# Six identity products behind the pack-query attention product of the first three head groups

## Chip, cores and metric

The kernel runs on one core of one Trainium2 chip. The metric is device time in microseconds (us); lower is better.

## What is computed

Attention through 32 packed queries per head, and two expert layers behind it:

```python
def sm_attn(qq, kk, vv):
    s = scale * np.matmul(qq, kk.transpose(0, 1, 3, 2))
    s = s - np.max(s, axis=-1, keepdims=True)
    a = np.exp(s)
    a = a / (np.sum(a, axis=-1, keepdims=True) + 1e-09)
    return np.matmul(a, vv)
p_packed = sm_attn(p, k, v)              # (4, 8, 32, 64)
out = sm_attn(q, p_packed, p_packed)     # (4, 8, 576, 64)
...
x = attn_out.transpose(0, 2, 1, 3).reshape(B * S, H * D)   # 2304 x 512
h = x @ w_in                             # d_ff 2048
g = np.maximum(h, 0.0) + np.log1p(np.exp(-np.abs(h)))
x = g @ w_out
gate = 1.0 / (1.0 + np.exp(-(x @ w_gate)))   # d_ff 1536
val = x @ w_val
return gate * val @ w_out2
```

## The kernel before

The four batches and eight heads are worked in eight units: unit u is batch u // 2 and four of its heads. `attn_unit(u)` is a generator of eleven stages, parted by `yield`. In order it transposes k (L347, copied out at L354), forms the scores of p (L378), takes their softmax (L386 to L398, the exponential on ScalarE at L389), transposes q (L347), transposes the softmax (L412, copied out at L413), multiplies it with v (L431), copies that product's blocks into `bdT` on ScalarE (L94, called from `copy`), forms the scores of q against `bdT` (L455), takes their softmax (L465 to L473, its last product on GpSimd), and, two empty stages later, transposes the result (L483) into `A2h` and `A2l` (L489 and L99).

The product with v goes to a PSUM tile `pp` of 128 x 512 float32, one bank, out of a pool of four (`bank1`). It fills columns 0 to 127; the copies into `bdT` read those. Columns 128 to 511 are not used.

`att_tick` runs one stage of one live unit. At the start, units 0 and 1 are run out by themselves, with unit 2 begun. From then on the stages of later units are put between the products of the first expert layer: `emit_h` (three products of split float32r parts, L111 to L113, on `Wp`, which `prep_wp_one` makes at L560 out of `bdT` and `w_in`), then abs, exp, ln on ScalarE (L613 to L615), the activation's end on VectorE (L623), and `emit_out1` (L641, L642, L644), summed on VectorE (L96 or L649). The weights come as float64 and are converted on VectorE (L178, L183, L187). The second expert layer follows, in Winograd's form (L111 to L113 again, by tile `bank`) with its output product at L965 to L967.

Each engine works through one queue in order. The queues' order is set when the program is built, out of the written order and the dependencies, and is not always the written one. An engine waits at a tile for the last instruction that it depends on.

Of the kernel before, what the change touches and what calls it, by code (L numbers as in the profile page):

```python
# [16 lines left out]
DRAM = bass.MemoryType.DRAM  # L17
# [3 lines left out]
def attn_moe_moe_kernel(  # L21
# [10 lines left out]
    w_out2: bass.AP,  # L32
    out: bass.AP,
):
    # float32 operands of the large products are split exactly into two
    # float32r parts (12 significant bits each): x = hi + lo, and a product is
    # hi*hi + hi*lo + lo*hi, accumulated in float32.
    #
    # The attention's second product is folded into w_in per batch:
    # (A2 @ pp) @ w_in = A2 @ (pp @ w_in), pp having 32 rows a head.  # L40
    #
    # Tokens of a batch are kept in the order (c, r) for token 6 r + c.
    nc = tc.nc
    B, H, S, D = q.shape
    NK = p.shape[2]
# [3 lines left out]
    P = 128  # L49
# [30 lines left out]
    cv = ctx.enter_context(tc.tile_pool(name="cv", bufs=NCV))  # L80
    wo_p = ctx.enter_context(tc.tile_pool(name="wo", bufs=4))

    # The layers' sums; queries, keys and values before those.
    xa = cst.tile([P, KD * NT], F32, name="xa")

    def bank2():
# [30 lines left out]
    att = tc.alloc_tile_pool(name="att", bufs=1, side="right")  # L117
    ph1 = tc.alloc_tile_pool(name="ph1", bufs=1, side="left")

# [1 line left out]
    # A weight's float64 words come as pairs of int32, in tiles of 512 columns.  # L121
    w32 = {
        nm: w.bitcast(I32)
        for nm, w in (
            ("in", w_in), ("out", w_out), ("g", w_gate), ("v", w_val), ("o2", w_out2)
        )
    }
    # Some of the second layer's are converted during the first and kept in DRAM.
    later = {f: [(nm, f // 2, f % 2) for nm in ("g", "v", "o2")] for f in range(2 * NCH2)}
    early = list(EARLY)  # L130
    order, early_in = [], {}
# [10 lines left out]
    def load_next():  # L142
        if not waiting:
            return
        nm, c, f = key = waiting.popleft()
        if XR and key == ("out", 0, 0):
            # The sums' tile is free until the first of them.
            t = xa[:, : 2 * DM].bitcast(I32).rearrange("p (n t) -> p n t", t=2)
        else:
            t = raw.tile([P, KD * P, 2], I32, tag="raw", name="raw_" + nm)  # L150
        a = c * CF + f * P
        if nm in ("out", "o2"):
            nc.sync.dma_start(t.rearrange("p n t -> p (n t)"), w32[nm][a : a + P, :])
        else:
            nc.sync.dma_start(
                t.rearrange("p (k n) t -> p k (n t)", k=KD),
                w32[nm][:, 2 * a : 2 * (a + P)].rearrange("(k p) x -> p k x", p=P),
            )
        raws[key] = t
# [1 line left out]
    cps = [CPS > 1]  # L161

    def convert(key, dst):
        # float64 -> float32 of the same value's leading 24 bits: sign and
        # exponent's first bit, seven bits of exponent with 20 of the mantissa,
        # three more of the mantissa.
        t = raws.pop(key)
        hw, lw = t[:, :, 1], t[:, :, 0]
        if len(dst.shape) == 3:
            hw = hw.rearrange("p (k n) -> p k n", k=KD)  # L170
            lw = lw.rearrange("p (k n) -> p k n", k=KD)
        to = x = dst.bitcast(I32)
        if cps[0] and dst.space != PSUM:
            x = bank1()
            if len(dst.shape) == 3:
                x = x.rearrange("p (k n) -> p k n", k=KD)
            x = x.bitcast(I32)
        nc.vector.tensor_scalar(  # L178
            x, hw, 3, 0x3FFFFFF8, op0=ALU.logical_shift_left, op1=ALU.bitwise_and
        )  # L180
        if not cps[0]:
            yield
        nc.vector.scalar_tensor_tensor(  # L183
            x, hw, -0x40000000, x, op0=ALU.bitwise_and, op1=ALU.bitwise_or
        )
        yield
        nc.vector.scalar_tensor_tensor(  # L187
            to, lw, 29, x, op0=ALU.logical_shift_right, op1=ALU.bitwise_or
        )
        load_next()  # L190
# [7 lines left out]
        split_lo(nc.gpsimd, lo, x, hi)  # L198
        return hi, lo

    # Queries, keys and values take the accumulators' slots before those are
    # needed; a slot's next tile is loaded behind its last use.
    PLACE = {
        0: "345", 1: "621", 2: "345", 3: "634", 4: "563", 5: "456",
        6: "565", 7: "656",
# [33 lines left out]
    def done_kqv(nm, u):  # L239
        for tag, key in list(busy.items()):  # L240
            if key == (nm, u):
                del busy[tag]
        load_kqv()

    # Work that goes in between the large products' instructions.
    jobs = deque()

    idle = deque()
# [9 lines left out]
        while any(nm == name for nm, _ in jobs):  # L258
            tick()

# [1 line left out]
    ident = cst.tile([P, P], F32, name="ident")  # L262
    make_identity(nc, ident)
    # lhsT of pp @ w_in: for a head pair, [2 heads x d, 2 batches x 2 heads x keys],
    # zero off a head's own block.
    bdT = ph1.tile([P, 2 * B + 2, P], F32, name="bdT")
    # lhsT of the scores of p: zero off a head's own block.
    pT = [att.tile([P, 4 * P], F32, name=f"pT{i}") for i in range(2)]
    for t in pT:
        nc.gpsimd.memset(t, 0.0)  # L270
    nc.gpsimd.memset(bdT, 0.0)

# [1 line left out]
    A2h = [big.tile([P, 2, S], F32R, tag="big", name=f"A2h{b}") for b in range(B)]  # L274
    A2l = [big.tile([P, 2, S], F32R, tag="big", name=f"A2l{b}") for b in range(B)]
    praw = {}
# [46 lines left out]
    RELD = 0  # L323
    SUMP = 0
    E1 = nc.scalar

    def heads(tile_, start, step):
        # Two blocks of 32 columns, a step apart.
        return tile_[:, start : start + 2 * step].rearrange("p (j x) -> p j x", x=step)[
            :, :, :NK  # L330
        ]

    def by_chunk(src, j):
        # Two heads of a chunk of tokens side by side.
        x = att.tile([CT, NC, 2, D], F32, tag="x", bufs=2, name="x")
        nc.gpsimd.tensor_scalar(
            x, src[:, 2 * j : 2 * j + 2].rearrange("p h c d -> p c h d"), 1.0, 0.0,
            op0=ALU.mult, op1=ALU.add,
        )
        return x  # L340

    def tr_pair(src, j, dst, eng):
        x = by_chunk(src, j)
        for hf in range(2):
            ps = bank1()
            for c in range(3):
                nc.tensor.transpose(  # L347
                    ps[:, c * CT : (c + 1) * CT],
                    x[:, 3 * hf + c].rearrange("p h d -> p (h d)"),
                    ident[:CT, :CT],  # L350
                )
            o = dst[:, j, hf * HS : (hf + 1) * HS]
            if eng is nc.scalar:
                eng.activation(o, ps[:, :HS], AF.Copy)  # L354
            else:
                eng.tensor_copy(o, ps[:, :HS])

    def attn_unit(u):
        b, g = divmod(u, 2)
# [60 lines left out]
        for j in range(2):  # L420
            for c in range(NC):
# [7 lines left out]
                for e in range(2):  # L429
# [6 lines left out]
                        stop=c == NC - 1,  # L436
                    )
        done_kqv("v", u)
        for e in range(2):
            r = slice(64 * e, 64 * e + 64)  # L440
            to = bdT[r].rearrange("p j n -> p (j n)")
            copy(
                BDA, heads(to, 512 * half + 256 * g + 64 * odd + 32 * e, 64 if odd else 192),
                heads(pp[r], 32 * e, 64),
            )
# [49 lines left out]
    live = []  # L495

    def att_left(u):
        # Stages until the units up to u are done.
        return sum(STAGES - n for _, n, x in live if x <= u) + STAGES * sum(
            x <= u for x in units  # L500
        )
# [7 lines left out]
        return n not in NEEDS or (NEEDS[n], u) in kqv  # L509

    def att_tick(last=2 * B):
        # Two units at a time, some stages apart.
        if units and ready(units[0], 0) and units[0] <= last and (
            not live or (len(live) < (NLV if last < 8 else 2) and min(x[1] for x in live) >= (G0 if len(live) == 1 and last < 8 else GP if last < 8 else GAP))
        ):
# [8 lines left out]
                    live.append(x)  # L524
                return

# [1 line left out]
    w_in_f, wo_hl, Wp = {}, {}, {}  # L528

    def x2(b, s):  # L530
        # The first layer's sums, transposed, for half a batch of tokens.
        i = KD * HS * (2 * b + s)
        return xa[:, i : i + KD * HS].rearrange("p (m t) -> p m t", m=KD)

# [122 lines left out]
                att_tick()  # L657
        tick()

    # The gates' and the values' products are one product [G V] = x2 [Wg Wv], by  # L660
    # halves of x2's columns and of a batch's tokens in Winograd's form with
    # seven products of halves:
    #   S1 = A21 + A22, S2 = S1 - A11, S3 = A11 - A21, S4 = A12 - S2
    #   T1 = B12 - B11, T2 = B22 - T1, T3 = B22 - B12, T4 = B21 - T2
    #   U = A11 B11 + S2 T2
    #   G1 = A11 B11 + A12 B21, V1 = U + S1 T1 + S4 B22
    #   G2 = U + S3 T3 + A22 T4, V2 = U + S3 T3 + S1 T1
    w2 = []
    NF = NCH2 * 2
    HB = B // 2  # L670
# [49 lines left out]
        split("S3", t)  # L720
        yield

    # A tile of the gates' and values' columns gives seven blocks of B: B11 and
    # B21, B22, T1 and T4, T3 and T2.
    def new_cv():
        return cv.tile([P, DM], F32, tag="cv", name="cv")

# [43 lines left out]
            yield  # L771

    def prep_B(ps, f):
        # The second pass reads the blocks back.
        if f in scratch:
            parts = [new_cv(), new_cv()[:, :CF], new_cv(), new_cv(), new_cv()]
            for x, a, n in places(parts):
# [16 lines left out]
            oh, ol,  # L794
        )

# [1 line left out]
    load_p(0, nc.scalar)  # L798
    load_kqv()
    for _ in range(4):  # L800
# [2 lines left out]
    n = 0  # L803
# [8 lines left out]
    jobs.append(("win1", prep_win(1)))  # L812
    jobs.append(("wp01", prep_wp_one(0, 1)))
    jobs.append(("wo1", prep_wo(1)))
    # Pairs of batches by columns; the first pair ends ahead of the other, which
    # leaves time for the second layer's preparation.
    entries = [(b, c) for b in range(B) for c in range(2)]
    groups = [(x, c) for c in range(2, NCH1 - 2) for x in range(2)]
    groups += [(x, c) for x in range(2) for c in range(NCH1 - 2, NCH1)]
# [52 lines left out]
                    between(m, ticks)  # L872
            pend.append((b, c, s))

# [1 line left out]
    if PRE:  # L876
        tc.keep_in_program_order(nc.scalar.preload_act_table_set("sigmoid_and_others"))
    while pend:
# [168 lines left out]
```

## Time and profile before

| | us |
|---|---|
| median of 3 runs | 874.49 |
| lowest, highest | 873.87, 879.49 |
| span of the profiled execution | 870.41 |
| TensorE busy in it | 841.8 (97%) |
| mean granted TensorE clock | 0.992 |

Of the profiled execution only its span, from the first to the last instruction, is known as its own time; the timed runs count what lies around the span as well, and are other executions. PE is TensorE's matmuls, PEld its weight loads, DVE VectorE, ACT ScalarE, POOL GpSimd, SP SyncE. Matmuls are pipelined, so a merged row's time counts the overlap of a product with the one ahead of it once, and the step from one start to the next is shorter than one product's time.

### The profile page before, as it was taken

What the parts mean: (1) busy time and instruction counts of PE and PEld (TensorE: products, weight loads), DVE (VectorE), ACT (ScalarE), POOL (GpSimd) and SP (SyncE); (2) the same over time, 40 slices, a digit from 0 to 9 for tenths busy, and PEclk for the clock granted to TensorE, in tenths of its full rate; (3) what the DMA queues carried; (4) which work ended last, traced back from release to release, by engine and by line L of the source; (5) the groups of instructions that cost most, each with busy time, mean ns of one, the idle gap of its engine ahead of it and who ended that gap; (6) DMA issues with size and microseconds to landing.
All of it is one profiled execution on the core that took longest, in us unless ns stands there. A gap on an engine that the chain in (4) does not pass through costs nothing.

```text
span 870.4 us, 15541 instructions
## 1 busy us (share of the span) xinstructions
PE 841.8 (97%) x6064; PEld 790.2 (91%) x6064; DVE 618.2 (71%) x1047; ACT 401.8 (46%) x721; POOL 473.4 (54%) x455
## 2 busy tenths in 40 slices
PE   6889999999999999999999999999989999999997
PEld 5778989989999999999989999999979999999995
DVE  2886556747476857758798688898898746667665
ACT  4557565656666656677633431232342432322210
POOL 4544333254646455476469787886983534436400
PEclk9979999999999999999999999999999999999999
DMA  9774320112032402310056555644424213213004
GB/s 242 197 207 113 83 66 19 49 49 73 25 98 91 134 1 98 110 43 1 2 154 193 162 168 153 188 128 150 153 75 143 82 47 92 67 43 109 14 1 109
DMA packets 58010, 85.55 MB, mean 98 GB/s; under 512 B 6353, under 2 KB 39249, under 8 KB 57937
## 3 DMA queue, kind: packets, MB, share of 16 engines
q1 hardware_dynamic: 57648, 84.49, 33.8%
q8 instruction: 48, 0.79, 0.4%
q14 instruction: 26, 0.20, 0.1%
q10 hardware_dynamic: 288, 0.07, 0.0%
HBM read 65.67 MB, written 18.87 MB: 97 GB/s over the span
## 4 chain that ended last, share of the span: by engine, by line
PE 81%; DVE 9%; DMA 3%; ACT 3%; POOL 2%; issue 1%; SPq 0%; DVEq 0%; ACTq 0%; POOLq 0%
PE bank L113 9%; PE bank L112 9%; PE bank L111 9%; PE ps L641 6%; PE ps L642 6%; PE ps L644 6%; PE ps L967 5%; PE ps L965 5%; PE ps L966 5%; PE ps L113 3%; PE ps L111 3%; PE ps L112 3%; PE ps L578 2%; PE ps L455 2%; DVE aop L99 2%
## 5 line engine op out<-in xcount | busy, mean ns | idle before, releaser
L111 PE MATMUL bank<-aop,BH 128*128 128x288 f32 x672 | 198.7, 296 | 2.8 <-DVE work L918 1.0
L112 PE MATMUL bank<-aop,BH 128*128 128x288 f32 x672 | 197.9, 295 | 1.0 <-DVE aop L99 0.9
L113 PE MATMUL bank<-aop,BL 128*128 128x288 f32 x672 | 198.7, 296 | 0.1
L99 POOL TENSOR_TENSOR ghl<-g,ghl 128x576 fp32r<-128x576 f32 x64 | 93.7, 1465 | 138.8 <-ACT ghl L106 134.4
L649 DVE TENSOR_TENSOR xa<-xa,ps 128x288 f32<-128x288 f32 x224 | 98.1, 449 | 76.9 <-PE ps L644 76.8
L641 PE MATMUL ps<-ghl,woh 128*128 128x288 f32 x512 | 149.2, 306 | 2.5 <-DVE xa L649 2.4
L642 PE MATMUL ps<-ghl,wol 128*128 128x288 f32 x512 | 143.9, 296 | 0.0
L111 PEld LDWEIGHTS bank<-aop,BH 128*128 128x128 f32 x672 | 126.2, 188 | 8.0 <-issue 1.2
L112 PEld LDWEIGHTS bank<-aop,BH 128*128 128x128 f32 x672 | 126.4, 188 | 5.1 <-DVE aop L99 1.6
L113 PEld LDWEIGHTS bank<-aop,BL 128*128 128x128 f32 x672 | 126.5, 188 | 0.4 <-POOL BL L99 0.4
L99 POOL TENSOR_TENSOR BL<-cv,BH 128x512 fp32r<-128x512 f32 (+1 forms) x96 | 117.6, 1241 | 7.2 <-ACT BH L106 6.1
L644 PE MATMUL ps<-ghl,woh 128*128 128x288 f32 x512 | 109.4, 295 | 0.0
L641 PEld LDWEIGHTS ps<-ghl,woh 128*128 128x128 f32 x512 | 96.9, 189 | 6.1 <-DVE xa L649 2.1
L642 PEld LDWEIGHTS ps<-ghl,wol 128*128 128x128 f32 x512 | 97.0, 190 | 0.5
L918 DVE TENSOR_TENSOR work<-work,bank 128x576 f32<-128x576 f32 (+1 forms) x100 | 71.0, 725 | 29.0 <-PE bank L113 28.4
L965 PE MATMUL ps<-oh,gv 128*128 128x512 f32 x216 | 84.6, 392 | 1.3 <-DVE xa L973 0.8
L966 PE MATMUL ps<-ol,gv 128*128 128x512 f32 x216 | 84.8, 393 | 0.0
L967 PE MATMUL ps<-oh,gv 128*128 128x512 f32 x216 | 84.7, 393 | 0.0
L644 PEld LDWEIGHTS ps<-ghl,woh 128*128 128x128 f32 x512 | 82.7, 189 | 0.0
L973 DVE TENSOR_TENSOR xa<-xa,ps 128x512 f32<-128x512 f32 x90 | 61.5, 683 | 27.4 <-PE ps L967 26.9
L947 ACT ACTIVATE work<-bank 128x576 f32<-128x576 f32 (+1 forms) x25 | 15.8, 633 | 137.2 <-DVE bank L918 137.2
L113 PE MATMUL ps<-A2h,wpl 128*128 128x288 f32 x256 | 76.3, 298 | 2.9 <-POOL wpl L99 2.0
(121 smaller groups left out, 1745.8 us busy)
## 6 DMA issues: line engine op xcount, KB each, us to landing
cv<-B SPq DMA_DIRECT2D x52, 256.0 KB, 2.7
B<-cv SPq DMA_DIRECT2D x48, 256.0 KB, 2.9
raw_in<-in_moe_w_in_dram SPq DMA_DIRECT2D x16, 512.0 KB, 4.0
raw_out<-in_moe_w_out_dram SPq DMA_DIRECT2D x16, 512.0 KB, 3.7
raw_g<-in_moe_w_gate_dram SPq DMA_DIRECT2D x12, 512.0 KB, 4.1
raw_v<-in_moe_w_val_dram SPq DMA_DIRECT2D x12, 512.0 KB, 4.4
raw_o<-in_moe_w_out_dram SPq DMA_DIRECT2D x12, 512.0 KB, 4.2
xa<-in_q_dram SPq DMA_DIRECT2D x6, 576.0 KB, 6.6
```

Of the source, the lines that this page charges most:

```text
L99: eng.tensor_tensor(lo, x, hi.bitcast(F32), op=ALU.subtract)
L111: nc.tensor.matmul(ps, wh, xh, start=first, stop=False)
L112: nc.tensor.matmul(ps, wh, xl, start=False, stop=False)
L113: nc.tensor.matmul(ps, wl, xh, start=False, stop=last)
L641: nc.tensor.matmul(out_, wh[:, ms], gh[:, f], start=f == 0, stop=False)
L642: nc.tensor.matmul(out_, wl[:, ms], gh[:, f], start=False, stop=False)
L644: nc.tensor.matmul(out_, wo_hl[c, f][0][:, ms], gl[:, f], start=False, stop=f == 1)
L649: nc.vector.tensor_tensor(dst, dst, out_, op=ALU.add)
L918: nc.vector.tensor_tensor(to, x, y, op=ALU.add)
L965: nc.tensor.matmul(bank, gh[:, ts_], oh, start=f == 0, stop=False)
L966: nc.tensor.matmul(bank, gh[:, ts_], ol, start=False, stop=False)
L967: nc.tensor.matmul(bank, gl[:, ts_], oh, start=False, stop=f == 1)
```

## The change

`WARM = 3` and a function `warm` are new. In units 0, 1 and 2, right behind the product with v and ahead of the copies into `bdT`, six products of the identity with itself (float32, 128 x 128 by 128 x 128) are written into the last 128 columns of `pp`. Nothing reads them. Comments of the file are blanked out, and nothing else changes.

```diff
     E1 = nc.scalar
+    WARM = 3
...
+    def warm(u, to, n):
+
+
+        if u < WARM:
+            for _ in range(n):
+                nc.tensor.matmul(to, ident, ident, start=True, stop=True)
 
     def attn_unit(u):
         b, g = divmod(u, 2)
...
                         stop=c == NC - 1,
                     )
         done_kqv("v", u)
+        warm(u, pp[:, 3 * P :], 6)
         for e in range(2):
             r = slice(64 * e, 64 * e + 64)
             to = bdT[r].rearrange("p j n -> p (j n)")
```

## Rows read from the trace of the kernel before

**Rows 1.** The page: span, and the granted TensorE clock in 40 slices.
```profile
span 870.4 us, 15541 instructions
...
PEclk9979999999999999999999999999999999999999
```

**Rows 2.** Windows of 25 us: busy time and count by engine, granted clock, DMA.
```profile
50.00:75.00 25.00, 23.46 (x203) 21.13 (x204) 18.67 (x41) 15.52 (x35) 11.84 (x11) 0.80 0.77 189
...
175.00:200.00 25.00, 23.01 (x153) 22.29 (x153) 12.29 (x24) 15.21 (x24) 11.95 (x11) 0.93 0.14 43
```

**Rows 3.** Windows of 0.5 us about the longer stretch at the lower clock.
```profile
50.00:50.50 0.50, 0.00 (x0) 0.00 (x0) 0.43 (x3) 0.50 (x2) 0.00 (x0) 0.70 0.05 18
...
60.00:60.50 0.50, 0.50 (x4) 0.50 (x3) 0.00 (x0) 0.43 (x1) 0.00 (x0) 0.56 1.03 223
```

**Rows 4.** Timeline of PE, 19 to 52 us: start, time, instructions, idle before.
```profile
19.87 1.24 PE L431 MATMUL ps<-a1T,xa 96*64 96x32 f32 x36 [0.39 <-ACT a1T L413]
21.85 0.86 PE L412 MATMUL ps<-ident,a 128*96 128x128 f32 x6 [0.73 <-DVE a L398]
...
24.65 1.59 PE L431 MATMUL ps<-a1T,xa 96*64 96x32 f32 x48
26.79 2.25 PE L455 MATMUL ps<-bdT,qT 128*96 128x64 f32 x24 [0.55 <-ACT bdT L94]
...
48.11 0.71 PE L347 MATMUL ps<-ident,x 96*128 96x96 f32 x6
51.52 4.10 PE L455 MATMUL ps<-bdT,qT 128*96 128x64 f32 x24 [2.69 <-ACT bdT L94]
```

**Rows 5.** The chain that ended last, 34 to 61 us: start, time, what.
```profile
34.26 0.84 POOL a L473
...
42.42 0.76 DVE g L623
...
55.62 0.96 PE ps L347 x6
...
56.60 1.51 PE ps L412 x6
58.11 1.91 PE ps L560 x8
60.02 0.54 PE ps L641
```

**Rows 6.** Timeline of ACT, 49 to 52 us.
```profile
49.10 0.74 ACT L389 ACTIVATE a<-ps,mx 128x576 f32<-128x576 f32 x1 [1.76 <-DVE mx L387]
...
50.41 0.20 ACT L94 ACTIVATE bdT<-ps 64x64 f32<-64x64 f32 x1
...
51.25 0.22 ACT L94 ACTIVATE bdT<-ps 64x64 f32<-64x64 f32 x1
```

**Rows 7.** The chain that ended last, later: the same products at the full clock.
```profile
96.07 2.01 PE ps L455 x24
98.08 0.50 PE ps L347 x6
99.89 0.66 PE ps L412 x6
...
155.67 1.04 PE ps L560 x8
...
170.31 0.86 PE ps L578 x4
```

**Rows 8.** The page, groups of instructions: a weight load of 128 x 128.
```profile
L111 PEld LDWEIGHTS bank<-aop,BH 128*128 128x128 f32 x672 | 126.2, 188 | 8.0 <-issue 1.2
```

**Rows 9.** Timeline of PE, two places: queue order at 61 us, a stall at 182 us.
```profile
61.45 0.29 PE L112 MATMUL ps<-A2l,wph 128*128 128x288 f32 x1
61.58 0.30 PE L641 MATMUL ps<-ghl,woh 128*128 128x288 f32 x1
...
182.27 0.40 PE L113 MATMUL ps<-A2h,wpl 128*128 128x288 f32 x1 [1.99 <-POOL wpl L99]
```

## Prediction

> **What bounds the kernel now.** I read the page first: the span, and the row of granted clocks [rows 1]. It is full nearly everywhere, but one slice early on shows 7 tenths. The windows of 25 us place what is lost: 0.80 of the clock between 50 and 75 us, and a smaller loss (0.93) between 175 and 200 us [rows 2]. From 75 us to the end TensorE is hardly ever idle, so time that it loses or gains early should arrive at the end: little behind it has slack. The finer windows put the drop inside the half microsecond from 50.0 (0.70 is full for 0.20 us and half for the rest, so at 50.20) and the return into the one from 60.0 (0.56, so near 60.44) [rows 3]. That is 10.2 us at 1.2 in place of 2.4 GHz.
>
> What stood ahead of the drop is in PE's own timeline [rows 4]: unit 2's transposes of q end at 48.82, and then TensorE is idle for 2.69 us, until the copies into bdT let the scores of q start at 51.52. The clock fell 1.4 us into that hole. The scores, transposes and weight products behind it ran at half speed, and the chain that ended last goes straight through them [rows 5]. ScalarE explains the hole [rows 6]: the product with v was done by 48.1, but the copies stand in ScalarE's queue behind an exponential that waits for VectorE until 49.10; they start at 50.41 and 51.25.
>
> The second loss is of the same kind: PE waits 1.99 us for GpSimd at 182.27 [rows 9], and the clock is low for some 3.4 us behind it (7% of a 25 us window at half is 14% of it [rows 2]). The change puts nothing there.
>
> **What one set of six costs.** The float32 products are two records each in this trace: unit 1's 24 products with v are x48, a unit's 12 products with bdT are x24 [rows 4]. So a set is 12 records of 128 moving columns with a 128 x 128 weight. The nearest rows at the full clock: four records of 256 columns in 0.86 us, so 0.108 us for 128 columns, and six transposes of 128 columns in 0.66 us, 0.11 us each [rows 7]. I take 12 x 0.11 = 1.3 us. The low end is the spacing of the smaller products against bdT, 2.01/24 = 0.084 us [rows 7], 1.0 us a set. The high end is a weight load that nothing hides, 0.188 us [rows 8], 2.3 us a set; I don't take it, since those loads lie under the products ahead of them.
>
> **Unit 0.** The product with v ends at 21.11 (19.87 + 1.24) and PE then waits 0.73 us for VectorE before unit 1's transposes [rows 4]. The set hides 0.7 of its 1.3 us in that wait; 0.6 us is left on the path. Ends: 0.3 and 1.6 us.
>
> **Unit 1.** The product with v ends at 26.24, and the scores of q start at 26.79 after the two copies [rows 4]. The only idle time is those copies' 0.55 us. If a copy may run while PE writes other columns of the same bank, the copies lie under the set, the scores start at 27.55, and the cost is 0.8 us. If the copies wait for the sixth product, the whole 1.3 us is added. I take 1.3 us: the copies are written behind the products and read the same tile, and the trace of before shows no engine reading a PSUM tile that PE is still filling. Ends: 0.5 (1.0 us a set, copies hidden) and 2.3 us.
>
> The Trainium skill bears on this in "PSUM — Partial Sum Buffer", section "PSUM bank collisions raise a hardware error": a write of TensorE and a read of ScalarE must not meet in one bank and quadrant. By that rule the copies have to be kept behind the set, 1.3 us rather than 0.8; no run here shows it yet.
>
> **Do those 1.9 us arrive?** Behind 26.79 the chain runs from the scores of q through the softmax (its last product on GpSimd at 34.26), into the first expert products, from their activation into VectorE's end of it at 42.42, and on through VectorE's and ScalarE's queues to the copies at 51.25 [rows 5, 6]. Each link there waits for the one ahead of it; none is a transfer that would come at a fixed time. I carry the 1.9 us through in full. Low end 0.9, if conversions of weights on VectorE slip into the wait.
>
> **Unit 2.** The product with v is done by 48.1, where q's transposes start [rows 4]; a set puts PE's end from 48.82 to about 50.1. The copies start at 50.41 because of what is ahead of them on ScalarE [rows 6], and q's transposes are copied out only behind the second copy at 51.25, so nothing waits: cost 0. The cover is ScalarE's queue; if it put the copies first, the set's 1.3 us would be on the path. What changes is the hole: 1.4 us (50.1 to 51.5) in place of 2.69, and it opens at about the point where the clock had fallen, not 1.4 us before it.
>
> **What the clock is worth.** On the chain the pieces at half clock are 4.10 (scores of q) [rows 4], 0.96, 1.51, 1.91 and 0.54 us [rows 5]: 9.0 us. At the full clock the same pieces are 2.01, 0.50, 0.66 and, for eight records of L560, 1.04 us [rows 7]; the last, a first product of a group, I halve to 0.3. That is 4.5 us, a difference of 4.5 us. With the scores done 2 us earlier, the transposes of q and of the softmax stand closer to ScalarE's copies of them; I take off 0.4 us for that wait. So 4.1 us if the clock stays up; the ends are 0 and 4.5.
>
> **Sum.** +0.6 +1.3 +0 -4.1 = -2.2 us. The profiled span is 870.41 us, and would be 868.2. The median of the runs, 874.49, lies 4.08 us above that span (the lowest run 3.46). I carry those 4.1 us over: 874.5 - 2.2 = 872.3 us.
>
> **Rivals.**
>
> (a) The clock falls all the same, and the kernel is slower. A hole of about 1.4 us is left in front of the scores of q, as the copies on ScalarE did not move. In the trace the clock dropped when PE had been idle for 1.4 us, which is just as long. For it: this near equality. Against it: holes of 0.73 and 0.55 us between the same kinds of products came without a fall [rows 4], and PE works without a break for longer ahead of the hole that is left. It decides from the point at which the hole left is again long enough for a fall. The price is the sets of units 0 and 1 with nothing in return, +1.9 us: 876.4.
>
> The Trainium skill, "TensorE: Matmul & The Clock Gate", section "What's actually happening", says that the point at which the clock changes is not tied to the kernel's start and differs between executions of one kernel. By that rule both (a) and my forecast would occur among the runs of one kernel, and the single profile of before cannot show how often; the spread of the runs of before, 873.87 to 879.49, is as wide as one such stretch (10.2 us at half, some 5 us) and agrees with it.
>
> (b) Another queue order. The order of PE's queue is not the written one: at 61.58 a product of the second weight stands among the three parts of the first [rows 9]. Eighteen more products can move what is built behind them. On the bad side the stall at 182 us, which costs 2.0 us of idle and, at half clock for 3.4 us, another 1.7, comes once more than now with the sets' cost: 874.5 + 1.9 + 3.7 = 880.1. On the good side that stall is gone on top of the forecast: 872.3 - 3.7 = 868.6.
>
> (c) The change does not do what it says: the products, which nothing depends on but the copies, are put elsewhere in PE's queue, say in front of a wait that hides them, or somewhere that leaves the hole. Then the time is that of before, 874.5. The write to pp ties them between the tile's first use and its release, so I give it little.
>
> **Chances.** My forecast 0.48; (a) 0.26; (b) bad 0.10, (b) good 0.11; (c) 0.05. The bounds of the unknown terms widen each of them: the forecast runs from 870.5 (0.3 and 0.5 on the path, 4.5 gained, gives 870.8) to about 874 (1.6 and 2.3 on the path and 4.1 gained gives 874.3), (a) from 875.4 to 878.4. A run of before can differ from another by 5 us. To leave out no more than 2 in 10 I go from 867.0, below (b) good, to 879.5, short of (b) bad. About what a measurement of this kernel can tell from no change is 1%, 8.7 us. Faster by over that means below 865.7: only (b) good with more than one stall gone, 0.04. Slower by over that means above 883.2: (b) bad with two more stalls, 0.05. Within: 0.91.
>
> **What would show it.** In the changed kernel's timeline of PE: twelve records behind each of the first three products with v, 1.3 us a set; unit 0's and unit 1's scores of q later by 0.6 and 1.9 us; the copies of unit 1 behind the set's last record; PE's idle time before unit 2's scores of q at 1.4 us; a granted clock of 1.00 from 50 to 65 us, and the scores of q there in 2.0 to 2.2 us rather than 4.1. The stall near 182 us and its low clock should stand as they do now. It would be wrong if the clock is low in that stretch again, if the sets cost 2 us each, or if waits appear behind 75 us that are not there now.

## The result

The changed kernel takes 868.33 us (median of 13 runs, 866.77 to 873.0); before it was 874.49 us in 13 runs beside them. The ratio is 0.9916, 95% interval 0.989 to 0.9941: faster by 0.6 to 1.1%. Run again beside other executions of before, it gave 867.84 us and 0.991 (0.9878 to 0.9943). The time lies in the forecast's range and the direction was right; the size was not, 6.2 us against 2.2. The change, 0.8%, is within the 1% that the forecast gave 0.91, though the interval reaches past it.

The page of the changed kernel, span and granted clock:

```profile
span 864.7 us, 15615 instructions
...
PEclk9999999999999999999999999999999999999999
```

Windows of 25 us (busy time by engine, granted clock, DMA), the two that lost clock in before [rows 2]:

```profile
50.00:75.00 25.00, 24.16 (x235) 21.79 (x234) 17.16 (x42) 16.34 (x39) 13.02 (x13) 1.00 0.82 193
175.00:200.00 25.00, 23.00 (x168) 22.38 (x167) 11.92 (x25) 15.29 (x25) 15.57 (x14) 1.00 0.13 41
```

Neither fall is there. The timeline of PE in the changed kernel answers to [rows 4]. Line numbers have moved: L364 is the new product, L439 the product with v, L464 the scores of q, L348 and L420 transposes.

```profile
20.12 1.24 PE L439 MATMUL ps<-a1T,xa 96*64 96x32 f32 x36 [0.40 <-ACT a1T L421]
21.29 1.60 PE L364 MATMUL ps<-ident 128*128 128x128 f32 x12
22.73 0.82 PE L420 MATMUL ps<-ident,a 128*96 128x128 f32 x6
...
27.20 1.60 PE L364 MATMUL ps<-ident 128*128 128x128 f32 x12
29.76 2.25 PE L464 MATMUL ps<-bdT,qT 128*96 128x64 f32 x24 [0.96 <-ACT bdT L94]
...
48.02 1.59 PE L439 MATMUL ps<-a1T,xa 96*64 96x32 f32 x48
49.54 1.60 PE L364 MATMUL ps<-ident 128*128 128x128 f32 x12
50.98 0.66 PE L348 MATMUL ps<-ident,x 96*128 96x96 f32 x6
52.31 2.25 PE L464 MATMUL ps<-bdT,qT 128*96 128x64 f32 x24 [0.67 <-ACT bdT L94]
54.40 0.66 PE L348 MATMUL ps<-ident,x 96*128 96x96 f32 x6
```

Each set is twelve records and 1.4 us from its start to the next instruction's. The hole ahead of unit 2's scores of q is 0.67 us, down from 2.69, and those scores take 2.25 us in place of 4.10. ScalarE's timeline in the changed kernel shows the copies into `bdT` behind the set:

```profile
22.99 0.45 ACT L94 ACTIVATE bdT<-ps 64x64 f32<-64x64 f32 x2 [2.33 <-PE ps L364]
...
28.84 0.22 ACT L94 ACTIVATE bdT<-ps 64x64 f32<-64x64 f32 x1 [2.38 <-PE ps L364]
...
51.83 0.43 ACT L94 ACTIVATE bdT<-ps 64x64 f32<-64x64 f32 x2
```

By the start times of the same instructions in the two profiles, the changed kernel is 0.25 us late before its first set (unit 0's product with v, 20.12 against 19.87), 0.88 late at unit 1's transposes of the softmax (22.73 against 21.85), 2.97 late at unit 1's scores of q (29.76 against 26.79), 0.79 late at unit 2's (52.31 against 51.52), and about 2.45 us early from 66 us on. That stays to 171 us. It becomes 4.0 us where before has its second low clock; PE's wait there is 2.00 us in the changed kernel too, and the clock does not fall behind it. Another 1.1 us comes near 211 us, where VectorE in before waits for a transfer of weights and in the changed kernel does not. The timelines of VectorE, first before, then the changed kernel:

```profile
211.49 0.69 DVE L178 TENSOR_SCALAR ps<-raw_out 128x512 int32<-128x512 int32 x1 [1.23 <-DMA raw_out<-in_moe_w_out_dram]
```
```profile
206.17 0.68 DVE L178 TENSOR_SCALAR ps<-raw_out 128x512 int32<-128x512 int32 x1
```

That transfer took 5.1 us from issue to landing in before and 3.6 us in the changed kernel. The like happens once more near 331 us and is worth 0.5 us. 2.45 + 1.55 + 1.1 + 0.5 makes 5.6 of the 5.7 us between the two spans.

### The profile page after: what moved, and what is told of

Its sections match the earlier page's. It is cut to its first block, busy times and chain, and to the rows that moved or that the text cites. A ratio compares the mean times of both kernels' runs of the same rounds, so it can differ in the third digit from the quotient of the medians.

```text
span 864.7 us, 15615 instructions
## 1 busy us (share of the span) xinstructions
PE 839.6 (97%) x6100; PEld 789.6 (91%) x6100; DVE 614.6 (71%) x1047; ACT 401.1 (46%) x721; POOL 473.2 (55%) x455
## 4 chain that ended last, share of the span: by engine, by line
PE 84%; DVE 7%; DMA 3%; ACT 2%; POOL 2%; issue 1%; SPq 0%; POOLq 0%; ACTq 0%; DVEq 0%
PE bank L113 9%; PE bank L111 9%; PE bank L112 9%; PE ps L650 7%; PE ps L651 7%; PE ps L653 7%; PE ps L976 5%; PE ps L975 5%; PE ps L974 5%; PE ps L113 4%; PE ps L111 4%; PE ps L112 4%; PE ps L587 2%; DVE aop L99 2%; PE ps L464 2%; PE ps L348 1%
```

## The experiments

All kernels are variants of the changed one, except the first. Each result gives every execution's mean granted clock beside its time, and that decides most of them. Places of a fall are known only for the profiled execution of each kernel. The table comes from the results; "low" is a mean clock below 0.987, "high" 0.996 and above (to three digits).

```
kernel                            median us  ratio to before (95%)     runs: low  between  high
before, beside all of these         875.02                               91:  26    61      4
changed                             868.33   0.9916 (0.9890-0.9941)      13:   0     2     11
changed, again                      867.84   0.9910 (0.9878-0.9943)       7:   0     0      7
before, again                       876.30   1.0010 (0.9982-1.0038)      12:   5     7      0
sets in units 0 and 1               870.05   0.9922 (0.9894-0.9950)       9:   0     7      2
sets in units 0 and 2               870.11   0.9953 (0.9927-0.9980)      12:   0     7      5
set in unit 0                       872.15   0.9970 (0.9949-0.9991)      12:   0    12      0
set in unit 1                       872.45   0.9980 (0.9947-1.0013)      12:   4     8      0
set in unit 2                       873.10   0.9979 (0.9948-1.0010)      12:   3     5      4
one column each                     878.16   1.0030 (1.0003-1.0058)      12:  11     1      0
sets in units 3, 4, 5               878.91   1.0038 (1.0010-1.0066)      12:   6     6      0
sets in banks of their own          871.91   0.9948 (0.9927-0.9969)      10:   0     3      7
one more set in the wait at 180     870.91   0.9941 (0.9916-0.9966)       8:   0     0      8
copies of unit 2 on VectorE         875.27   0.9988 (0.9961-1.0014)      12:   4     8      0
```

**Before, again.** No edit.

> The kernel of before once more, to see how its granted clock varies between executions. Theory A (the gain is TensorE's clock: a stretch at half speed near 50 us, and at times one near 183 us, that the products of unit 2 prevent): the mean granted clock is below 0.995 in nearly every run, 0.988 to 0.994, and the median is 874.5 us within 1. Theory B (the gain is the order of the queues, which is rebuilt when products are added; the clock is incidental): nothing else than the same time; the clock may be near 1.000 in many of the runs without their being faster.

876.3 us, clocks 0.982 to 0.992: 0.8 us above what theory A allowed, with lower clocks than it named in five of twelve. Over the 91 executions of before, the 26 low ones have a median of 880.0 us at 0.9815, the 61 between 874.2 at 0.991, the 4 high ones 870.3 at 0.996. The clock is not incidental: it orders the executions by time, over 10 us. This profile has a fall that mine of before had not. Windows and PE's timeline of before in this execution:

```profile
20.00:25.00 5.00, 3.58 (x59) 3.31 (x57) 4.03 (x9) 2.64 (x9) 0.10 (x1) 0.79 1.05 271
25.00:30.00 5.00, 4.45 (x74) 4.27 (x74) 2.91 (x7) 1.54 (x5) 1.52 (x2) 0.87 0.91 256
50.00:55.00 5.00, 2.31 (x51) 2.09 (x48) 4.66 (x11) 3.20 (x9) 0.48 (x1) 0.86 0.61 156
...
185.00:190.00 5.00, 4.52 (x23) 4.52 (x24) 0.91 (x2) 2.02 (x3) 4.16 (x4) 0.68 0.00 2
```
```profile
23.05 1.52 PE L412 MATMUL ps<-ident,a 128*96 128x128 f32 x6 [1.03 <-DVE a L398]
```

An early fall, 3.4 us from about 22.9 us, starts inside the wait behind unit 0's product with v: 1.03 us here, 0.73 in [rows 4].

This execution, at 0.989, is not one of the low ones. Its three falls make 17 us at half speed. A mean of 0.9815 takes some 32 us (an estimate: 2 x 0.0185 x 870). No low execution of before was profiled, so where the other 15 us lie no trace shows. That they belong to the early fall is inferred, from the variants in which unit 0's set takes the low executions away.

**Only unit 2.**
```diff
-        if u < WARM:
+        if u == 2:
```

> Only unit 2 has the six products. Theory A: the clock stays up from 50 to 60 us as in the changed kernel, and the sets of units 0 and 1 (0.8 us late at unit 2's scores of q in the changed kernel) are saved: 867.5 us, between 866 and 868.5. Theory B: the order of the first two units is that of before, so some of the gain goes: 869 to 874.

873.1 us: a miss for theory A by 5 us, and inside what theory B gave. The clock does stay up at unit 2's scores of q, with a hole of 1.40 us ahead of them. Four of twelve executions are at 0.996 or above, against 4 of 91 of before. But three of twelve are low, so what makes an execution low remains, and in the profile a wait at another place has a fall of 6.8 us behind it, from about 62.4 us:

```profile
61.72 0.40 PE L113 MATMUL ps<-A2h,wpl 128*128 128x288 f32 x1 [2.00 <-DVE wpl L99]
...
62.76 0.44 PE L113 MATMUL ps<-A2h,wpl 128*128 128x288 f32 x1
```

The second row is the same kind of product at half speed (0.44 against 0.29 us).

**Only units 0 and 1.**
```diff
-    WARM = 3
+    WARM = 2
```

> Units 0 and 1 have the six products, unit 2 has none. Theory A: the hole ahead of unit 2's scores of q is back and with it the half clock near 50 us; the two sets are paid for nothing: 875.5 us, between 874.5 and 877, mean clock below 0.995. Theory B: the queues are rebuilt from unit 0 on, as in the changed kernel, so most of the gain stays: 867 to 871.

870.05 us: theory A as I had put it falls. It had these two sets as a mere price, and they bring most of the gain. Theory B's number came true, but the clocks speak for a wider theory: no execution is low, and the fall near 50 us is shorter (6.8 us in the profile, from 52.0), behind a hole of 1.24 in place of 2.69 us:

```profile
51.56 3.73 PE L464 MATMUL ps<-bdT,qT 128*96 128x64 f32 x24 [1.24 <-ACT bdT L94]
```

**All three, one column each.**
```diff
-                nc.tensor.matmul(to, ident, ident, start=True, stop=True)
+                nc.tensor.matmul(to[:, :1], ident, ident[:, :1], start=True, stop=True)
```

> All eighteen products are there, but each moves one column instead of 128, so that the waits and very nearly the queue order of the changed kernel stay and the work is gone. Theory A: nothing fills the hole, the clock falls near 50 us: 874 us, between 872.5 and 875.5, clock below 0.995. Theory B: 867 to 869, and rather below the changed kernel, since the price of the products is gone.

878.16 us, slower than before and above what either theory gave. I had missed one thing, that these products take as long as the full ones:

```profile
21.11 1.50 PE L364 MATMUL ps<-ident 128*128 128x1 f32 x12
...
26.91 1.89 PE L364 MATMUL ps<-ident 128*128 128x1 f32 x12
29.34 4.11 PE L464 MATMUL ps<-bdT,qT 128*96 128x64 f32 x24 [0.54 <-ACT bdT L94]
```

So this kernel pays the price of all three sets, and the clock falls all the same, near 28, near 55 and, like the last one of before, near 188 us. Windows of the first two:

```profile
25.00:30.00 5.00, 4.46 (x70) 4.27 (x69) 2.47 (x7) 1.48 (x4) 0.41 (x1) 0.78 0.98 242
...
55.00:60.00 5.00, 4.04 (x26) 3.75 (x26) 3.46 (x8) 3.52 (x9) 0.92 (x1) 0.52 0.69 209
```

The expectation took it that this kernel has the changed kernel's queue order. It has not. Listed by start time in the traces, with the sets left out, the instructions of TensorE, VectorE, ScalarE and GpSimd come in exactly the order of before. The changed kernel's lists differ from that by 194 lines on TensorE, some 100 each on VectorE and ScalarE, and 34 on GpSimd. ScalarE's copies into `bdT` of unit 2 show it. They stand apart, with an activation between them, as in [rows 6], where the changed kernel has them together behind all three activations (51.83, above):

```profile
56.09 0.20 ACT L94 ACTIVATE bdT<-ps 64x64 f32<-64x64 f32 x1
...
56.93 0.22 ACT L94 ACTIVATE bdT<-ps 64x64 f32<-64x64 f32 x1
```

So this run says nothing against theory B. It is a clean comparison with before: the same order, eighteen narrow products more, a ratio of 1.003 (1.0003 to 1.0058), and the clock low in 11 of 12 executions against 26 of 91.

**Units 3, 4 and 5.**
```diff
-        if u < WARM:
+        if 3 <= u < 6:
```

> The three sets of six stand in units 3, 4 and 5, where TensorE has little idle time, and none in units 0 to 2. Theory A (the time follows the granted clock; the falls near 22 to 28, near 50 and near 183 us are what the sets prevent): all falls of before stay, and three sets of 1.5 us are on TensorE's path: 879 us, between 876.5 and 881, clock 0.98 to 0.993. Theory B (any rebuilt queue order of this kind is better than that of before): below 873.

878.91 us, as theory A has it: the falls of before stay. At like clocks the price can be read: its six executions at 0.990 to 0.992 have a median of 876.3 us against 874.6 for the 47 of before at these clocks, its six low ones 882.1 against 880.0. Three sets of 1.4 us cost 1.7 to 2.1 us there. Against theory B the run says little: its order hardly differs from that of before (26 lines on TensorE, 4 on GpSimd).

**Sets in banks of their own.**
```diff
-        warm(u, pp[:, 3 * P :], 6)
+        if u < WARM:
+            warm(u, bank1()[:, :P], 6)
```

> As the changed kernel, but each set writes a PSUM bank of its own, so that the copies into bdT no longer wait for it. Theory A: the same clock, and in units 0 and 1 the copies run under the set; the scores of q of unit 1 start some 1 us earlier: 867.3 us, between 866 and 868.5. A rival (the copies' wait costs nothing, later work hides it): 868.3, as the changed kernel. If the clock falls more often than there: 870 to 873.

871.91 us: neither the gain nor the tie came. The copies no longer wait, and unit 1's scores of q start 2.96 us behind the start of its product with v (24.89), in place of 4.09 us (25.67 to 29.76) in the changed kernel. But GpSimd's order is another, and a hole of 2.34 us opens a little later, with a fall of 6.8 us behind it:

```profile
27.85 2.17 PE L465 MATMUL ps<-bdT,qT 128*96 128x64 f32 x24
...
36.75 0.47 PE L493 MATMUL ps<-ident,a 96*128 96x96 f32 x3 [2.34 <-POOL a L483]
```

Being early was worth nothing: by 107 us this profile is 3.3 us behind the changed kernel's.

**One more set in the wait near 180 us**, nine products between the second and third part of the first product of that stage:
```diff
+                if (b, c, s, f, t) == (0, 2, 0, 0, 0):
...
+                    warm(0, ps[:, 1, 384:], 9)
```

> As the changed kernel, and nine more identity products, into unused columns, inside the 2.0 us for which TensorE waits near 180 us. Theory A: the fall of 3.4 us behind that wait, which most runs of the changed kernel seem to have (mean clock 0.998), is gone: mean clock 0.999 to 1.000 in most runs, 867.2 us, between 866 and 868. Rival (that fall costs next to nothing, or the products come too late to fill the wait): 868 to 869.

The clock came out as theory A said, 0.999 or 1.000 in seven of eight executions. PE's timeline shows 0.65 us of the wait left:

```profile
177.27 2.17 PE L364 MATMUL ps<-ident 128*128 128x128 f32 x18
180.09 0.40 PE L623 MATMUL ps<-A2h,wpl 128*128 128x288 f32 x1 [0.65 <-POOL wpl L99]
```

The time, 870.91, did not: in the profiles it is 0.3 us behind the changed kernel up to 170 us and 4.2 behind in the second expert layer, in three steps (near 180, 287 and 446 us). PE's waits for VectorE's sums rise from 1.5 to 2.7 us. What sets those steps off is open; a full clock does not by itself make the shorter time.

**Copies of unit 2 on VectorE, no products.**
```diff
-    WARM = 3
+    WARM = 0
...
-                BDA, heads(to, 512 * half + 256 * g + 64 * odd + 32 * e, 64 if odd else 192),
+                BDA and u != 2, heads(to, 512 * half + 256 * g + 64 * odd + 32 * e, 64 if odd else 192),
```

> No products at all; the copies of unit 2 into bdT are VectorE's, in whose queue they stand ahead of the softmax's later steps, so that the hole ahead of unit 2's scores of q gets shorter by itself. Theory A: the fall near 50 us goes or gets shorter and the early one near 22 us stays as in before: 871.5 us, between 869 and 874. Rival (the fall comes from the kinds of products there, not from the hole): 873.5 to 875.5, clock 0.991 as before.

875.27 us, no gain that can be told from none. The hole is 1.43 us and the clock falls in the profile from 50.6 for 6.8 us, in place of 10.2; four of twelve executions are low. The rival's time came (873.5 to 875.5), and theory A's shorter fall. The hole is about half as long, and the clock still falls, 0.5 us behind its end.

**The changed kernel again, and single sets.**

> The changed kernel once more, beside runs of before on the chip of these four, for its granted clocks. If the time follows the clock: mean clock 0.998 in most runs and 868.5 us, between 867 and 870, 6 to 7 us under before. If the first result was luck of a few runs: 870 or more.

867.84 us, all seven executions at 0.998 or 1.000.

```diff
-        if u < WARM:
+        if u == 0:
```

> Only unit 0 has its six products. Theory (before has an early fall near 22 us, in the wait of 0.7 to 1.0 us between unit 0's product with v and unit 1's transposes, and unit 0's set fills just that wait): the early fall is gone, the one near 50 us stays: 870.5 us, between 869 and 873, clock 0.993 or 0.994 in most runs and hardly any at 0.985 or below. Rival (the early fall starts behind unit 1): as before, 874 to 876, with clocks of 0.985 and below in a third of the runs.

872.15 us, as expected, and no execution low: unit 0's set alone takes those away. The late fall stays in full, behind 3.16 us:

```profile
52.26 4.11 PE L464 MATMUL ps<-bdT,qT 128*96 128x64 f32 x24 [3.16 <-ACT bdT L94]
```

```diff
-        if u < WARM:
+        if u == 1:
```

> Only unit 1 has its six products. Theory of unit 0's wait: the early fall stays, 874.5 to 877, with clocks of 0.985 and below in some runs. Rival (the early fall starts behind unit 1): 870 to 871.5, clock 0.993 or 0.994.

872.45 us, better than its theory, but four of twelve executions are low and the early fall stands in the profile (3.4 us from 21.7). What unit 1's set does is seen later: the hole ahead of unit 2's scores of q is 1.24 us, as with units 0 and 1. Between that set and the hole lies another queue order, on VectorE above all (told below).

```profile
21.71 1.51 PE L420 MATMUL ps<-ident,a 128*96 128x128 f32 x6 [1.11 <-DVE a L406]
...
51.90 3.71 PE L464 MATMUL ps<-bdT,qT 128*96 128x64 f32 x24 [1.24 <-ACT bdT L94]
```

```diff
-        if u < WARM:
+        if u in (0, 2):
```

> Units 0 and 2 have their sets, unit 1 has none: both falls are covered, and the set with the highest price (the scores of q of unit 1 were 3.0 us late behind it) is saved. Theory: 867 us, between 866 and 868.5, clock 0.998 and above. Rival (that price is hidden under the load of k, which the same stretch of GpSimd's queue waits for, and a hole opens there instead): 869 to 872, with a fall near 35 us.

870.11 us, the rival's number, though not by the rival's hole: without unit 1's set the hole ahead of unit 2's scores of q is 1.85 us even with unit 2's own, and in the profile the clock falls 2 us behind its end, for 3.4 us.

```profile
52.01 2.35 PE L464 MATMUL ps<-bdT,qT 128*96 128x64 f32 x24 [1.85 <-ACT bdT L94]
```

No variant beats the change. Units 0 and 1 alone come within its interval (0.9922 against 0.9916 and 0.9910), so that unit 2's set adds to the time saved is seen in the clocks (7 of 9 executions at 0.994 or 0.995, against 2 of 20), not told by the medians.

Theory B, that the gain is the queue order, has its test in two of these. Unit 0's variant has nearly the order of before (GpSimd the same, 6 lines on VectorE, 22 on ScalarE, 28 on TensorE), and its low executions are gone: that is the set and not the order. Unit 1's variant is nearer to the changed kernel's order than to that of before (from the changed kernel 6 lines on GpSimd, 22 on VectorE, 32 on ScalarE, 134 on TensorE; from before 32, some 100, 104 and 172), and most of the gain is missing, with four executions low. So the order without the sets of units 0 and 2 is not enough. But unit 1's set works through the order that it brings, so the two are not wholly parted.

## Why the prediction was right in direction and short in size

**What bounds the kernel.** Right: the time follows TensorE's clock, and time lost in the first 60 us arrives at the end. The 91 executions of before show it better than the one profile I had. The 4.1 us that I carried over from span to median are not a constant: every execution's time lies 1.7 to 2.3 us above its own span. The rest was that the profiled execution was a short one. The forecast of the change does not hang on it.

**What a set costs.** Right: 1.4 us, against 1.3. It does not leave out the copies: they wait for the sixth product, as I took it (ScalarE's rows above). The rule of the Trainium skill on PSUM bank collisions, in "PSUM — Partial Sum Buffer", agrees with that wait; with a bank of their own the copies did not wait.

**Units 0 and 1 as a price of 1.9 us, carried through in full.** This is the step that failed first. From the start of unit 0's product with v, 0.25 us of the lateness being older, unit 0's set cost 0.63 us, as I had it. Unit 1's cost 2.0, more than my 1.3: its set took 1.5, and the wait for the copies grew from 0.55 to 0.96, as the second copy came behind a step of the softmax on ScalarE (28.84 and 29.49). But nothing of the 2.97 us was left at unit 2's exponential on ScalarE, which starts at 49.11, against 49.10 in [rows 6]. VectorE's timelines show where it went, first before, then the changed kernel, and below them ScalarE's in the changed kernel:

```profile
42.42 0.76 DVE L623 SCALAR_TENSOR_TENSOR g<-ps,t 128x576 f32<-128x576 f32 x1 [0.42 <-ACT t L615]
...
44.53 1.79 DVE L187 SCALAR_TENSOR_TENSOR w_in<-raw_in,w_in 128x512 int32<-128x512 int32 x1
46.24 1.50 DVE L178 TENSOR_SCALAR w_in<-raw_in 128x512 int32<-128x512 int32 x1
47.67 0.74 DVE L386 TENSOR_REDUCE mx<-ps 128x1 f32<-128x576 f32 x1
```
```profile
42.97 1.65 DVE L187 SCALAR_TENSOR_TENSOR w_in<-raw_in,w_in 128x512 int32<-128x512 int32 x1
45.32 0.76 DVE L632 SCALAR_TENSOR_TENSOR g<-ps,t 128x576 f32<-128x576 f32 x1 [0.69 <-ACT t L624]
...
46.53 0.76 DVE L394 TENSOR_REDUCE mx<-ps 128x1 f32<-128x576 f32 x1
```
```profile
49.11 0.74 ACT L397 ACTIVATE a<-ps,mx 128x576 f32<-128x576 f32 x1 [2.21 <-DVE mx L395]
```

The activation's end is still 2.90 us late (45.32 against 42.42), and the softmax's maximum behind it is 1.14 us early (46.53 against 47.67). In before, conversions of weights stand between the two. In the changed kernel most of them are done ahead of the activation's end, while VectorE would have waited. That is the low end I had named and not taken, conversions that slip into the wait. It left nothing of the lateness, where my low end left 0.9 us. It comes with another order of VectorE's queue. The profiles of unit 1's variant and of units 0 and 1 show the same; those of unit 0, of unit 2 and of both do not.

**Unit 2, cost 0.** The 0.79 us that the scores of q are late there are not left over from the earlier sets. In the two variants with unit 1's set but not unit 2's, the copies on ScalarE stand between the activations, in units 0 and 1 at 50.44 and 51.29. With unit 2's set they stand behind all three, at 51.83. So that set cost some 0.8 us, through ScalarE's queue. The hole follows: 2.69 - 1.43 (TensorE later at unit 2's product with v, 48.02 against 46.59) - 1.44 (the set) + 0.79 (the scores later) = 0.61, measured 0.67.

**The hole left, 1.4 us, and rival (a).** The hole was 0.67, for the reason just given. Rival (a) is nearer than its 0.26 in the variants: behind holes of 1.24 and 1.43 us with no set of unit 2 ahead the clock fell, and with the sets of units 0 and 2, behind 1.85 us, too. Had unit 1's set been the mere price that I took it for, (a) would have come in part. The hole's length does not decide alone: in the profile of unit 2's variant no fall came behind 1.40 us. What decides is not shown.

**What the clock is worth, 4.1 us.** Nearly right for the fall that I costed: the changed kernel goes from 0.79 us late at the scores to 2.45 early behind 66 us, 3.2 us in place of 4.1. The sum up to there, -2.45, is close to my -2.2 by luck: the price was 1.1 us smaller than I had it, and the gain 0.9. What was mis-sized is the number of falls. Before has up to three: near 22, near 50 and near 183 us. The first is not in the profile that I read, and I took the third as untouched. Unit 0's set takes the low executions away, and with them, as I read it, the first fall (none of 71 executions low in the kernels that have that set at full width, 26 of 91 in before, 3 to 6 of 12 in the variants without). The third went in the profile, 1.55 us, and in the changed kernel's seven later executions the clock was 1.000 in four, 0.998 in three, though PE's wait there stands at 2.0 us. One fall of 3.4 us makes 0.998 (an estimate: 1.7 of 870 us), so about half of the changed kernel's executions may still have one. The Trainium skill ("TensorE: Matmul & The Clock Gate", "What's actually happening") says that where the clock changes differs from execution to execution; the runs agree, 0.981 to 0.996 for one and the same kernel. I cited this and still made the sum from one execution.

**Another order (b).** Its good side gave 868.6 us, almost the time measured, but by another mechanism: the stall of 2.0 us that was to go still stands, and only the low clock behind it went. What came otherwise is worth 1.6 us in favour in the profiles (near 211 us, a transfer that landed in 3.6 us and not 5.1, and the like near 331), and more than that against in the variant with one more set. Why the transfer is faster is open. Of the profiles, the three of kernels without any products show the wait near 211 us (1.23, 1.10 and 0.70 us), and none with products does. The one-column kernel, in the order of before, is without it too, so it is not the order alone. How much is left to the order can be estimated from the executions of before: each 0.01 of mean clock goes with 6 to 7 us, which carried on to 0.998 gives 869.0 to 870.2 us. The changed kernel's nine executions there have a median of 869.0. So at like clocks it is ahead by 0 to 1.2 us of the 6.2.

## What to carry to other kernels

Where TensorE waits for other engines in a stretch of small products, look at the granted clock in several executions before summing what a stall costs: a profile shows the falls of one. Work that nothing reads can pay, if it stands in the waits that it fills, and its lateness may vanish in the next wait; check by a version that keeps the instructions and takes their width away. Compare the order of every queue in the two traces before calling such a version clean: here the narrow one got the order of before. Take each set out by itself: which one is "only a price" was guessed wrongly here.

## What the runs showed of the hardware

Six float32 products of one column took as long as six of 128 columns, 1.5 us and 1.6 us for twelve records, and did not keep the clock up: its mean was below 0.987 in 11 of 12 executions, against 26 of 91 in before with the same queue order. The full products, in another order, had none of 20.

ScalarE's copies out of columns 0 to 127 of a PSUM bank waited for six products written into columns 384 to 511 of it: unit 1's first copy started at 28.84 us, where the product with v had ended at 27.26 and the six ended at 28.80. With the products in a bank of their own the copy started at 26.53, right behind the product with v (26.48).
